# Transposing x by crossbar DMA in place of TensorE, in a convolution and token-mixing kernel

## The chip, the cores and the metric

One core of one Trainium2 chip. The metric is the device time of one execution in microseconds (us). Every time, ratio and profile in this document is from runs in the "fast" state, so no comparison mixes states; one of the four runs of h2_act (1607.5 us) was in the slow state and is left out. A "ratio" is the mean time of one kernel's runs over the mean of the other's runs of the same rounds, so it isn't quite the ratio of the medians that are quoted beside it.

Engines: PE is TensorE (matmul), PEld its weight loads, DVE VectorE, ACT ScalarE, POOL GpSimd. SPq is the SyncE queue that issues DMA. A crossbar transfer is a DMA with `transpose=True`. A transfer lands when its data have arrived; landing times are counted from its issue. A halo copy brings a chunk the 16 rows of history that its convolution needs. "L138" is line 138 of that kernel's file; the change moves later lines by some ten, so L408 of the kernel before is L417 of the changed one.

## The reference

```python
def _attn_ref(x, weight):                  # x (8, 4224, 192), weight (8 heads, 7 taps)
    w = softmax(weight)                    # cut: written out in the original
    x_pad = concat([zeros(6 rows), x])     # causal
    x_unf = x_pad[:, idx, :].reshape(B, S, K, H, group)
    return einsum('hk,bskhg->bshg', w, x_unf)

def _moe_ref(x, w_theta, w_tok_r, w_tok_i, w_ch):
    theta = x @ w_theta                                  # contracts over the channel
    zr, zi = x * cos(theta), x * sin(theta)
    y = einsum('ts,bsd->btd', w_tok_r, zr) + einsum('ts,bsd->btd', w_tok_i, zi)
    u = x + y
    return u + maximum(u @ w_ch, 0.0)                    # contracts over the channel
```

The large work is the token mixing: two 4224 x 4224 matrices times 1536 columns. The theta product contracts over the channel, and x comes out of the convolution with tokens on the partitions, so x must be transposed before it. That transpose is what the change touches.

## The kernel before

The 4224 tokens are 33 chunks of 128. A chunk is loaded, convolved, transposed, multiplied by `w_theta`, and turned into seven combinations z, which the mixing matmuls (`y`) read. Eleven chunks are alive at a time. Chunks 0 to 10 are prepared in an opening; chunks 11 to 32 are prepared in two later stages, spread as events between mixing matmuls. Preparation uses the PSUM pool "mm" (two buffers).

```python
    def transposed(u, by_dve=False):
        tp = banks("tp", F16)
        for k in range(6):
            pe(nc.tensor.transpose(
                tp[:, 0, k * P : (k + 1) * P], u[:, k * P : (k + 1) * P], ident))
        uT = wk.tile([P, 6, P], F16, name="uT", tag="uT")          # 2 buffers
        evacuate(uT[:, :, :].rearrange("p k s -> p (k s)"), tp[:, 0, 0 : 6 * P], by_dve)
        return uT

    class Chunk:
        def __init__(self, k, before=None):
            ...                                   # for a in range(4), a quarter each:
                if before is not None:            # 16 rows of history, SBUF to SBUF
                    nc.sync.dma_start(out=hist, in_=before.xw[lo + Q : lo + Q + HALO, h, :, :])
                ...
                nc.gpsimd.dma_start(out=self.xw[...], in_=x[...])  # x from HBM, cast to f16

        def conv(self, j):
            ...                                   # 8 matmuls, evacuated by ACT into self.x
            if j == 1:
                for a in range(NQ):
                    t0 = token(self.k, a)
                    nc.sync.dma_start(out=xs[t0 : t0 + Q, :], in_=self.x[a * Q : (a + 1) * Q, :])

        def transpose(self, g):                   # g = 0, 1: the two halves of the batch
            self.xT[g] = transposed(self.x[:, g * GC : (g + 1) * GC], ...)

        def theta(self, g):
            v = channel_mix(self.xT[g], wth)      # 8 matmuls on PE
            ...                                   # two sines on ACT into z

    # later chunks: places in a step, in sevenths of it, for
    # conv, conv, transpose, transpose, theta, theta, product, product, sums, sums
                pos = [0, .5, 1.3, 1.6, 2.1, 2.5, 3.1, 3.15, 3.4, 3.6]
                ...
                at += 2.3                         # the second chunk of the same step

    # the opening, iteration i: ch is chunk i, old is chunk i - 1; between(n) puts
    # mixing matmuls in between, as far as there are any
        ch.conv(0); between(2); old.theta(0); between(1); ch.conv(1)
        between(2); old.theta(1); between(1)
        ch.transpose(0); old.product(Z11); between(1)
        ch.transpose(1); old.product(Z21); ...
```

## Time and profile before

| | before |
|---|---|
| time | 1469.05 us median of 4 runs (1468.66 to 1469.96) |
| PE busy | 1434.6 us, 98% of the span |
| transposes of x on PE | 66 groups of six |
| landing of stores of x (96 KB, SP queue) | median 4.5 us from issue |

The chain of waits in order of time (start, duration, what), kernel before, in a later stage, and one long piece of it:

```profile
107.54 315.09 PE y L408 x1938
...
437.57 0.34 PE tp L153 x6
437.91 0.65 PE y L408 x4
438.56 0.34 PE tp L153 x6
438.89 1.62 PE y L408 x10
```

Six transposes cost the chain 0.34 us. The unbroken stretches of 315 and 296 us are useful landmarks: they hold no chunk work, so the time up to the first one's end is the opening, from there to the second one's end is the first later stage, and the rest follows.

### The profile page before, as it was taken

The page shows a single profiled execution, that of the slowest core. Times are in us where ns is not written, and L with a number is a line of the kernel's source. Part 1 is how long each engine was busy: PE and PEld are TensorE (multiplying, and loading weights), DVE is VectorE, ACT ScalarE, POOL GpSimd, SP SyncE. Part 2 cuts the span into 40 slices and gives each one's busy share as a digit, 9 for nine tenths or more (in the row PEclk, how much of TensorE's full clock was granted, in tenths as well). Part 3 has the DMA queues.
Part 4 walks back from the last instruction along what each step waited for, and adds up shares of the span by engine and source line. Part 5 has one row for each costly group of instructions (what it writes and reads, how often), then busy time and mean ns, then how long its engine had stood idle before and what let it go on. Part 6 is the DMA issues. An engine that isn't in the chain of part 4 may idle for free.

```text
span 1469.8 us, 24434 instructions
## 1 busy us (share of the span) xinstructions
PE 1434.6 (98%) x10095; PEld 905.6 (62%) x10095; DVE 1001.0 (68%) x1050; ACT 360.7 (25%) x461; POOL 430.3 (29%) x659
## 2 busy tenths in 40 slices
PE   7789999999999999999999999999999999999997
PEld 4556666666666666666666666666666666666665
DVE  6884655454548687766656658769777787778575
ACT  6861101111134353000000015254122222121224
POOL 7422211111223322211113232332233333453220
PEclk9999999999999999999999999999999999999998
DMA  9976756574699999887879989999778777999873
GB/s 172 227 155 145 144 104 144 96 151 89 149 232 212 232 224 263 193 198 167 209 162 239 200 194 229 201 232 256 128 191 197 173 182 185 224 237 217 196 201 108
DMA packets 234975, 274.16 MB, mean 187 GB/s; under 512 B 69104, under 2 KB 202608, under 8 KB 234864
## 3 DMA queue, kind: packets, MB, share of 16 engines
q0 software_dynamic: 163616, 95.30, 49.0%
q1 hardware_dynamic: 71248, 177.30, 34.1%
q8 instruction: 79, 1.29, 0.3%
q14 instruction: 32, 0.26, 0.1%
HBM read 245.49 MB, written 111.28 MB: 243 GB/s over the span
## 4 chain that ended last, share of the span: by engine, by line
PE 91%; DVE 3%; ACT 3%; DMA 1%; issue 1%; POOL 0%; DVEq 0%; ACTq 0%; POOLq 0%
PE y L408 81%; PE v L138 6%; PE tp L153 3%; ACT z L233 2%; PE pc L196 2%; DMA st<-in_moe_w_tok_i_dram 1%; DVE pv L373 1%; DVE z L244 1%; DVE z L238 0%; DVE wt L308 0%; DVE pv L437 0%; ACT uT L148 0%; DVE wt L320 0%; ACT pv L371 0%; ACT z L148 0%
## 5 line engine op out<-in xcount | busy, mean ns | idle before, releaser
L408 PE MATMUL y<-z,wt 128*128 128x384 f16 x7656 | 1295.3, 326 | 7.7 <-DVE pv L373 6.8
L408 PEld LDWEIGHTS <-wt 128*128 128x128 f16 x7656 | 737.5, 98 | 475.0 <-issue 10.4
L373 DVE TENSOR_TENSOR pv<-y,pv 128x768 f32<-128x768 f32 x324 | 308.5, 953 | 374.2 <-PE y L408 348.6
L308 DVE STREAM_TRANSPOSE wt<-st 128x1408 f16<-128x1408 f16 (+7 forms) x224 | 326.4, 1463 | 7.7 <-DMA st<-in_moe_w_tok_i_dram 7.0
L295 POOL DMA_DIRECT2D st<-in_moe_w_tok_i_dram x232 | 132.7, 581 | 497.7 <-DVE wt L308 473.7
L295 POOL DMA_DIRECT2D st<-in_moe_w_tok_r_dram x232 | 132.7, 581 | 459.0 <-DVE wt L308 443.7
L320 DVE TENSOR_TENSOR wt<-wt 128x1408 f16<-128x1408 f16 (+7 forms) x216 | 204.1, 945 | 9.5 <-PE y L408 6.6
L148 ACT ACTIVATE uT<-tp 128x768 f16<-128x768 f16 x127 | 102.3, 813 | 296.8 <-PE tp L153 294.9
L148 ACT ACTIVATE z<-pc 128x768 f16<-128x768 f32 x65 | 52.9, 814 | 386.5 <-PE pc L196 386.5
L371 ACT ACTIVATE pv<-y 128x768 f32<-128x768 f32 x66 | 53.7, 813 | 281.5 <-PE y L408 281.5
L138 PEld LDWEIGHTS <-uT 128*128 128x128 f16 x1056 | 93.0, 99 | 25.9 <-issue 9.9
L437 DVE SCALAR_TENSOR_TENSOR pv<-v,pv 128x768 f32<-128x768 f32 x66 | 62.7, 949 | 46.8 <-PE v L138 45.5
L183 POOL DMA_DIRECT2D xw<-in_x_dram x132 | 76.5, 591 | 35.8 <-issue 10.1
L427 ACT ACTIVATE ub<-pv 128x768 f16<-128x768 f32 x66 | 54.8, 837 | 90.6 <-DVE pv L373 89.5
L244 DVE TENSOR_TENSOR z<-z 128x768 f16<-128x768 f16 x132 | 73.4, 556 | 3.8
L233 ACT ACTIVATE z<-v,half_pi 128x768 f16<-128x768 f32 x66 | 59.6, 903 | 40.0 <-PE v L138 39.8
L238 DVE TENSOR_TENSOR z<-z 128x1536 f16<-128x1536 f16 x66 | 60.4, 950 | 10.8 <-ACT z L233 10.8
L355 POOL TENSOR_TENSOR pv<-pv,xr 128x1536 f32<-128x1536 f32 x20 | 62.9, 3144 | 7.9 <-issue 4.5
L138 PE MATMUL v<-wch,uT 128*128 128x192 f16 x528 | 56.9, 254 | 3.5 <-DVE pv L437 1.9
L138 PE MATMUL v<-wth,uT 128*128 128x192 f16 x528 | 54.3, 246 | 3.1 <-ACT z L233 3.0
L233 ACT ACTIVATE z<-v 128x768 f16<-128x768 f32 x66 | 53.2, 805 | 0.0
L153 PE MATMUL tp<-ident,z 128*128 128x128 f16 x396 | 33.4, 222 | 8.8 <-ACT z L233 8.3
(43 smaller groups left out, 201.5 us busy)
## 6 DMA issues: line engine op xcount, KB each, us to landing
part<-pv SPq DMA_DIRECT2D x79, 768.0 KB, 4.3
pv<-part SPq DMA_DIRECT2D x79, 768.0 KB, 5.4
out_dram<-pv SPq DMA_DIRECT2D x66, 384.0 KB, 4.5
st<-in_moe_w_tok_r_dram POOLq DMA_DIRECT2D x136, 176.0 KB, 5.8
st<-in_moe_w_tok_i_dram POOLq DMA_DIRECT2D x136, 176.0 KB, 4.9
xs<-z SPq DMA_DIRECT2D x132, 96.0 KB, 4.5
xw<-in_x_dram POOLq DMA_DIRECT2D x121, 96.0 KB, 5.9
part<-xs POOLq DMA_DIRECT2D x26, 384.0 KB, 7.4
```

The costliest lines, as they stand in the source:

```text
L138: pe(nc.tensor.matmul(v[:, k, b * D : (b + 1) * D], lhsT=tT[:, 3 * k + b + i, :], rhs=w[:, 2 * b + i, :], start=(i == 0), stop=(i == 1),))
L148: act(nc.scalar.activation(out=out, in_=in_, func=AT.Copy))
L153: pe(nc.tensor.transpose(tp[:, 0, k * P : (k + 1) * P], u[:, k * P : (k + 1) * P], ident))
L183: nc.gpsimd.dma_start(out=self.xw[lo : lo + n, h, :, :], in_=x[:, t0 : t0 + n, :].rearrange("b s d -> s b d"),)
L233: act(nc.scalar.activation(**args))
L244: dve(nc.vector.tensor_tensor(out=z[:, o, :], in0=z[:, a, :], in1=z[:, b, :], op=ALU.subtract))
L295: pool(nc.gpsimd.dma_start(out=st[a * Q : (a + 1) * Q, 0:nb, :, 0:n] .rearrange("i r bt s -> i (r bt) s"), in_=w[self.tbs[0] * P : (self.t ...
L308: dve(nc.vector.transpose(self.w[name][:, 0 : self.n, :, :], self.st[int(name[1])][:, int(name[0]) - 1, :, 0 : self.n * Q] .rearrange("p b ...
L320: dve(nc.vector.tensor_tensor(out=self.w[name][:, 0 : self.n, :, :], in0=self.w[a][:, 0 : self.n, :, :], in1=self.w[b][:, 0 : self.n, :, : ...
L355: pool(nc.gpsimd.tensor_tensor(out=self.pv[i], in0=self.pv[i], in1=xr, op=ALU.add))
L373: dve(nc.vector.tensor_tensor(out=o, in0=yv, in1=o, op=ALU.add))
L408: pe(nc.tensor.matmul(y[cn][:, q, 0:BH], lhsT=self.w[wn][:, c, :, :].rearrange("p bt i -> p (bt i)"), rhs=chunks[k].z[:, zn, q * BH : (q + ...
```

## The change

The intent is to take the 396 transposes of x from the bound engine and the evacuations from ACT, and to let the DMA crossbar do them, SBUF to SBUF. The stores of x go behind the transfers on the same queue, theta is moved later, uT gets four buffers, and `wt` gives up one to pay for it. The transposes of u at the end of the kernel stay on TensorE.

```diff
+    def turned():
+        return wk.tile([P, 6, P], F16, name="uT", tag="uT", bufs=4)
+
+    def crossed(u):
+        uT = turned()
+        nc.sync.dma_start(out=uT, in_=u, transpose=True)
+        return uT
...
-            if j == 1:
-                for a in range(NQ):              # the store, cut
+        def store(self):                         # the same four transfers
...
         def transpose(self, g):
-            self.xT[g] = transposed(
-                self.x[:, g * GC : (g + 1) * GC], 0 < self.k < 3 or (self.k, g) == (0, 1)
-            )
+            self.xT[g] = crossed(self.x[:, g * GC : (g + 1) * GC])
...
-            return wpool.tile([P, NW, NQ, Q], F16, name="wt", tag="wt", bufs=11)
+            return wpool.tile([P, NW, NQ, Q], F16, name="wt", tag="wt", bufs=10)
...
-                pos = [0, .5, 1.3, 1.6, 2.1, 2.5, 3.1, 3.15, 3.4, 3.6]
+                pos = [0, .4, .8, .81, .82, 2.6, 3.0, 3.6, 3.65, 3.9, 4.1]
...                                              # the opening, behind ch.conv(1):
+        if ch:
+            for g in range(NG):
+                ch.transpose(g)
+            ch.store()
...                                              # and away from their old places
-        if ch:
-            ch.transpose(0)
```

More of the change, by code (lines that the diff above doesn't have):

```diff
@@ L155, in transposed @@
             ))
-        uT = wk.tile([P, 6, P], F16, name="uT", tag="uT")
+        uT = turned()
         evacuate(uT[:, :, :].rearrange("p k s -> p (k s)"), tp[:, 0, 0 : 6 * P], by_dve)
@@ L209, in conv @@
             )
-            if j == 1:
-                for a in range(NQ):
-                    t0 = token(self.k, a)
-                    nc.sync.dma_start(
-                        out=xs[t0 : t0 + Q, :], in_=self.x[a * Q : (a + 1) * Q, :]
-                    )
+        def store(self):
+            for a in range(NQ):
+                t0 = token(self.k, a)
+                nc.sync.dma_start(
+                    out=xs[t0 : t0 + Q, :], in_=self.x[a * Q : (a + 1) * Q, :]
+                )
         def transpose(self, g):
-            self.xT[g] = transposed(
-                self.x[:, g * GC : (g + 1) * GC], 0 < self.k < 3 or (self.k, g) == (0, 1)
-            )
+            self.xT[g] = crossed(self.x[:, g * GC : (g + 1) * GC])
         def theta(self, g):
@@ L253, in tasks @@
                 yield lambda g=g: self.transpose(g)
+            yield self.store
             for g in range(NG):
@@ L642 @@
         between(1)
-        if ch:
-            ch.transpose(0)
         if old:
             old.product(Z11)
-        between(1)
-        if ch:
-            ch.transpose(1)
+        between(2)
         if old:
```

## The prediction

> **What bounds the kernel now.** TensorE: the page gives PE 98% busy of 1469.8 us, and the chain of waits is 91% PE. Busy time by windows shows PE full through nearly all of 150 to 1400 us. It falls short in the opening (36.0 of the first 50 us, 43.4 of the next) and at the end. Every TensorE instruction taken out of the dense part is real time. In the opening, where eleven chunks are prepared one after another, the chain alternates between PE, ACT and DVE, at 6.7 to 7.9 us a chunk.
>
> **What is removed.** 396 transposes of x, in 66 groups of six. The chain in order of time shows a group taking 0.34 us of PE in the dense part. All 66 make 22.4 us; the 44 of chunks 11 to 32 make 15 us. That is 1.5% at most. 66 evacuations of 0.81 us on ACT (five are 0.56 us on DVE) and 66 uses of the two "mm" PSUM slots also go. In the opening ACT is about 85% busy (42.7 of 50 us), so 1.6 us a chunk could matter: PE waits 8.3 us for a sine before a transpose.
>
> **What is added.** 66 crossbar transfers of 192 KB on the SP queue. No trace here has one. The Trainium skill, "VectorE: DVE Perf Modes", section "The three transpose paths", gives 1309 ns for one 128x128 by crossbar; no run here shows it. Ordinary transfers on this queue take a median 4.3 us (48 KB, SBUF to SBUF) to 4.6 us (stores of 96 KB) to land. My estimate, from those landings and the skill's figure (six tiles, partly parallel), is 5 to 8 us from x complete to the first xT landed, the second 1 to 3 us later.
>
> **What lies on the critical path.**
> - Later chunks: theta now comes 1.8 sevenths of a step (about 6.5 us, a step being 26.7 us) behind the transfers. That roughly covers one landing. I expect -15 us, with 0 to 10 us given back in stalls before theta.
> - Opening: theta(0) still follows in the next iteration. The timeline shows the x evacuation ending at 74.4 us and the next theta(0) at 78.4 us: 4.1 us of room, less than an estimated landing. [...] the shortfall stalls everything. The cycle theta, sine, evacuation, transfer, theta would be about 4.5 us plus the landing, 10 to 11 us instead of 7.7, over ten chunks: +15 to +35 us, after the removed work.
> - The stores of x move behind the transfers; nothing early needs them. wt with 10 buffers instead of 11: at most 9 or 10 are alive, so about 0.
>
> Sum: about +10 us, most likely 1479 us. Range 1442 to 1570. Faster by over 2% 0.04 (the ceiling is the 22 us plus part of 20 us of idle PE), within 2% 0.58, slower 0.38.
>
> **What would show it.** Right: the unbroken 300 us stretch of L408 in the chain starts later than the present 107.5 us; PE waits for DMA uT<-z before L138 in the first 110 us, 1 to 4 us each; between 420 and 580 us the step falls from 26.7 to about 25.4 us; the ACT group uT<-tp falls from 127 to 66. Wrong: no PE wait on uT in the opening (then about 1447 us), or waits of several us at nearly every theta in the dense part.
>
> **What would make it wrong.** A crossbar transfer much dearer than a plain one: at 8 us or more of the SP queue or the engines, two per 13 us fill it and hold up pv and halo loads: 1550 us or beyond. Or landing within 4 us, which leaves nearly the whole gain. A third risk: the added small packets delay the W loads.

## More of the kernel before

The kernel before was run again with each group of experiments, with medians of 1468.9 to 1470.5 us.

Engine totals, then three rows of the span cut into 40 slices (busy tenths; PEclk is the clock granted to TensorE; DMA is the mean busy share of the 16 DMA engines), then the DMA queues, from the page of the kernel before:

```profile
PE 1434.6 (98%) x10095; PEld 905.6 (62%) x10095; DVE 1001.0 (68%) x1050; ACT 360.7 (25%) x461; POOL 430.3 (29%) x659
...
PE   7789999999999999999999999999999999999997
...
PEclk9999999999999999999999999999999999999998
DMA  9976756574699999887879989999778777999873
...
q0 software_dynamic: 163616, 95.30, 49.0%
q1 hardware_dynamic: 71248, 177.30, 34.1%
```

PE is full except in the first three slices and the last. But the DMA row is at 9 in the same places where chunks are prepared: the first two slices, slices 12 to 16 and 25 to 28, among others. The quiet stretch from slice 3 to 11 is at 4 to 7. q1, the queue that the crossbar transfers will join, has 71,248 packets.

Busy time by windows (PE, PEld, DVE, ACT, POOL; then granted clock, DMA share, GB/s), kernel before: the opening, and the first later stage.

```profile
0.00:108.00 108.00, 86.33 (x774) 57.06 (x775) 84.36 (x137) 76.69 (x102) 54.63 (x105) 1.00 1.04 187
422.00:577.00 155.00, 154.27 (x1223) 99.00 (x1222) 116.96 (x141) 69.28 (x88) 46.37 (x82) 1.00 0.99 230
```

The DMA share is 1.04 and 0.99: it sums the queues' packet times, so it can pass 1.

## The result, and the profile after

The changed kernel takes 1527.97 us (median of 4, 1521.68 to 1531.41) against 1469.05: ratio 1.0395 (95% interval 1.0361 to 1.043), slower. Its output is correct.

The page of the changed kernel, same lines:

```profile
PE 1438.2 (94%) x9701; PEld 892.1 (58%) x9701; DVE 1001.0 (66%) x1045; ACT 314.4 (21%) x400; POOL 430.3 (28%) x659
...
PE   6669999999998998999999999898999999999997
...
PEclk9889999999999999999999999999899999999999
DMA  9997765656599999988788989999977787899974
...
q0 software_dynamic: 163616, 95.30, 47.9%
q1 hardware_dynamic: 124048, 190.29, 40.0%
```

394 instructions are gone from PE, and yet it is busy for 3.6 us longer. Its idle time (span less busy) went from 35.2 to 87.8 us. q1 moves only 13 MB more (66 times 192 KB), in 52,800 more packets, and its share of 16 engines rises from 34.1% of 1469.8 us to 40.0% of 1526.0 us. That is 109 us more, or an estimated 1.65 us of all 16 engines per transfer.

The same windows by stage, changed kernel, and two pieces of the chain:

```profile
0.00:130.00 130.00, 91.89 (x641) 55.91 (x642) 81.43 (x132) 64.94 (x85) 54.62 (x105) 0.88 1.15 190
445.00:619.00 174.00, 154.04 (x1096) 93.56 (x1096) 117.94 (x141) 51.69 (x66) 46.01 (x82) 0.97 1.12 226
```
```profile
130.06 315.08 PE y L417 x1938
...
485.49 10.21 DMA uT<-z
495.70 0.05 issue
495.74 0.88 PE v L138 x8
```

The first unbroken stretch begins at 130.1 us in place of 107.5. In the later stage the same work takes longer at a higher DMA share and a lower clock, and the chain now runs through a transfer that takes 10.21 us.

Who PE waited for (us in total, times, longest), and the issues and landings of the new tile, changed kernel:

```profile
PE v L138 <- DMA uT<-z: 63.4, 28, 8.1
...
L156 SPq DMA_TRANSPOSE uT<-z x66: 1211/1324/3937, 12.8 to 1073.7; - x66
...
DMA to landing us min/median/max: 2.5/6.4/12.3
```

63.4 us of the idle time is theta waiting for its own transposed x. A transfer takes 1.3 us to issue and a median 6.4 us to land, 12.3 at worst.

Why PE's busy time didn't fall is seen in PE's timeline around the longest wait (idle time in brackets) and in the windows there:

```profile
92.92 0.82 PE L417 MATMUL y<-z,wt 128*128 128x384 f16 x4
101.81 1.46 PE L138 MATMUL v<-wth,uT 128*128 128x192 f16 x8 [8.07 <-DMA uT<-z]
103.06 0.85 PE L417 MATMUL y<-z,wt 128*128 128x384 f16 x2
...
109.72 0.82 PE L417 MATMUL y<-z,wt 128*128 128x384 f16 x4
```
```profile
102.00:108.00 6.00, 6.00 (x35) 3.98 (x34) 1.98 (x2) 2.90 (x4) 0.18 (x1) 0.56 0.21 59
108.00:118.00 10.00, 8.97 (x76) 5.63 (x74) 9.40 (x14) 6.41 (x9) 2.72 (x5) 1.00 1.10 175
```

After the 8.07 us pause eight theta matmuls take 1.46 us instead of 0.82, and the granted clock of the next 6 us is 0.56; then it is back at 1.00. With these pauses the mean granted clock over the whole run fell from 0.996 to 0.980, which is some 24 us of 1526 by that figure. It agrees with the busy time: 22.4 us of transposes are gone and the sum is 3.6 us higher, so the rest became about 26 us slower. The Trainium skill, "TensorE: Matmul & The Clock Gate", section "Why this matters for your kernels", advises no PE-idle gaps of over about 3 us between matmul bursts. This trace agrees roughly. Of the waits for uT, those of 8.07, 4.59, 4.14, 3.54 and 3.08 us were followed by a theta of 1.46 us. Behind those of 4.58 and 3.09 us theta itself took 0.88 and 0.83 us, but what came next was slow: the clock of 496 to 500 us was 0.57, and eight matmuls of the convolution took 0.85 us in place of 0.52. Just below 3 us it goes both ways: two waits of 2.97 us were followed by slow matmuls, those of 2.94 and 2.88 us were not. One wait of only 1.56 us was followed by a theta of 1.46 us, but a pause of 1.82 us had ended 1.2 us before it began.

### The profile page after: what moved, and what is told of

It is laid out like the page before. It is cut to its first block, busy times and chain, and to the rows that moved or that the text cites. A ratio compares the mean times of both kernels' runs of the same rounds, so it can differ in the third digit from the quotient of the medians.

```text
span 1526.0 us, 23663 instructions
## 1 busy us (share of the span) xinstructions
PE 1438.2 (94%) x9701; PEld 892.1 (58%) x9701; DVE 1001.0 (66%) x1045; ACT 314.4 (21%) x400; POOL 430.3 (28%) x659
## 4 chain that ended last, share of the span: by engine, by line
PE 78%; DMA 14%; DVE 3%; ACT 2%; issue 1%; POOL 1%; SPq 0%; DVEq 0%; POOLq 0%; ACTq 0%
PE y L417 71%; DMA uT<-z 11%; PE v L138 5%; DMA xw<-in_x_dram 2%; ACT z L241 1%; PE tp L162 1%; PE pc L205 1%; DVE pv L382 1%; DMA st<-in_moe_w_tok_i_dram 1%; DVE z L252 1%; POOL st L304 1%; DVE wt L317 1%; DVE pv L446 0%; ACT z L148 0%; POOL xw L192 0%
## 5 line engine op out<-in xcount | busy, mean ns | idle before, releaser
L329 DVE TENSOR_TENSOR wt<-wt 128x1408 f16<-128x1408 f16 (+7 forms) x216 | 204.0, 944 | 22.1 <-PE y L417 18.2
L138 PEld LDWEIGHTS <-uT 128*128 128x128 f16 x1056 | 96.2, 104 | 97.0 <-DMA uT<-z 75.9
L138 PE MATMUL v<-wth,uT 128*128 128x192 f16 x528 | 65.1, 276 | 64.9 <-DMA uT<-z 63.4
L148 ACT ACTIVATE uT<-tp 128x768 f16<-128x768 f16 x66 | 53.2, 810 | 242.1 <-PE tp L162 242.1
L205 PE MATMUL pc<-xw,bands 96*64 96x192 f16 x528 | 38.5, 271 | 4.7 <-DMA xw<-in_x_dram 3.4
```

Of the source, the lines that this page charges most:

```text
L138: pe(nc.tensor.matmul(v[:, k, b * D : (b + 1) * D], lhsT=tT[:, 3 * k + b + i, :], rhs=w[:, 2 * b + i, :], start=(i == 0), stop=(i == 1),))
L148: act(nc.scalar.activation(out=out, in_=in_, func=AT.Copy))
L329: dve(nc.vector.tensor_tensor(out=self.w[name][:, 0 : self.n, :, :], in0=self.w[a][:, 0 : self.n, :, :], in1=self.w[b][:, 0 : self.n, :, : ...
```

## The experiments

The theories. **Wait**: theta stands too close behind a transfer that needs 6 us to land; with more distance PE would not wait and the 15 us of the later stages would be won. **Load**: the DMA engines are full where chunks are prepared; the transfers lengthen everything there, wherever theta stands. **Queue**: it is the SP queue, by its issue time (1.3 us a transfer) or by transfers waiting for earlier ones to land.

All with three rounds of the kernel before beside them. Stage columns are differences to the kernel before, worked out from the ends of the two unbroken stretches and the span of the profiled run (before: 422.6, 449.8 and 597.4 us), each good to some 0.1 us. By the 2% verdict e2, e7, h1 and h3 count as the same and e6 and g3 as unclear, but the 95% interval of every ratio lies above 1.

| run | median us | ratio | up to the end of stretch 1 | to the end of stretch 2 | rest |
|---|---|---|---|---|---|
| the change | 1528.0 | 1.0395 | +22.5 | +18.3 | +15.3 |
| e2_opening_only | 1491.1 | 1.0144 | +23.5 | 0.0 | -4.4 |
| e3_later_only | 1503.0 | 1.0224 | +0.8 | +18.2 | +12.2 |
| e4_unread | 1518.7 | 1.0337 | +17.5 | +16.5 | +9.3 |
| e7_copy | 1489.6 | 1.0140 | +13.4 | +1.6 | +2.5 |
| g1_unread_halo | 1508.6 | 1.0270 | +18.8 | +9.2 | +9.8 |
| g2_halo | 1527.7 | 1.0386 | +22.4 | +18.7 | +15.5 |
| e6_far_open_pe | 1500.7 | 1.0206 | -0.3 | +12.6 | +18.2 |
| g3_far_halo_open_pe | 1497.6 | 1.0195 | +0.8 | +9.6 | +13.8 |
| h1_quiet | 1484.1 | 1.0102 | +13.4 | 0.0 | -0.6 |
| h2_act | 1585.4 | 1.0816 | +38.1 | +38.7 | +37.1 |
| h3_half | 1480.3 | 1.0087 | +0.8 | +3.5 | +5.0 |
| c256 | 1514.4 | 1.0284 | +20.5 | +15.2 | +8.6 |

### Which stage: e2_opening_only and e3_later_only

```diff
-            self.xT[g] = crossed(x)
+            self.xT[g] = crossed(x) if self.k < NW else transposed(x)      # e2
+            self.xT[g] = crossed(x) if self.k >= NW else transposed(x, ...) # e3
```
In each, the part that went back to TensorE also went back to its places of before.

> The crossbar for chunks 0 to 10 only; chunks 11 to 32 are transposed on TensorE at the places of before. By the markers of the two traces the opening alone ends 22.5 us later in the changed kernel, so 1491 us if the stages add up. If the loss sat in the later stages through the shared queue, this stays near 1470.

> The reverse: the opening as before, the crossbar for chunks 11 to 32 at the places of the change. The markers give +34.6 us for the two later stages, so 1503 us if the stages add up. My prediction had 1454 to 1464 for this half (-15 us and 0 to 10 us of stalls).

They gave 1491.1 us (ratio 1.0144) and 1503.0 us (1.0224). The stages add up roughly: about 21 and 33 us, of the 59 of the whole. (The 34.6 us in the second expectation don't agree with the table: the markers give 18.3 and 15.3.) The opening's loss is of the size predicted. The later stages' is not: 33 us lost, where 5 to 15 us of gain was predicted.

One more effect shows here. e2 has no crossbar after the opening, and yet its rest is 4.4 us shorter than before. It has four buffers of uT, which the transposes of u at the end use too. From the end of the last mixing matmul to the end of the span it is 18.0 to 19.3 us in all four profiles with two buffers of uT (the kernel before, e4, g1 and h1) and 14.4 to 15.0 us in all ten with four. So the change gains some 4 us at its end, which the prediction didn't have, and its transfers cost that much more; no run changed the buffers alone.

### The transfers without anyone waiting for them: e4_unread

```diff
+    def unread(u):
+        uX = wk.tile([P, 6, P], F16, name="uX", tag="uX", bufs=2)
+        nc.sync.dma_start(out=uX, in_=u, transpose=True)
 ...                                    # kernel before, wt with 10 buffers, in conv(1):
             if j == 1:
+                for g in range(NG):
+                    unread(self.x[:, g * GC : (g + 1) * GC])
                 for a in range(NQ):    # the stores, as before
```

> The kernel before, all transposes on TensorE, plus all 66 crossbar transfers at the places of the change, into tiles that nobody reads, stores of x behind them, wt with 10 buffers. Theory of the wait (theta stands too close behind a transfer that needs 6 us to land): nothing waits, so 1469 to 1476 us. Rival, contention (the transfers load the SP queue and the DMA engines and hold up halo copies, x loads and weights): 1500 us or more, with PE waiting for xw or wt.

1518.7 us (ratio 1.0337): some 48 us for transfers that nobody reads. The theory of the wait alone falls here. The change loses 59 us although it saves an estimated 22.4 us of transposes, some 81 us in all; by this estimate 48 of them come without anyone waiting for uT, if the two parts add up. Who PE waited for, and the landings, in this run:

```profile
PE pc L200 <- DMA xw<-xw: 11.9, 6, 2.7
...
DMA to landing us min/median/max: 2.5/6.8/12.0
```

PE now waits for the halo copies of the next chunk, for outputs that DVE was late with, and so on. No single wait explains the loss; it is spread. In the profiled run idle time rose by 25.2 us and busy time by 18.2 us, the latter with the granted clock at 0.983. One flaw: the unread tiles had two buffers only, so the SP queue itself waited 15.0 us for them.

### The same bytes as a plain copy: e7_copy

```diff
-        nc.sync.dma_start(out=uT, in_=u, transpose=True)
+        nc.sync.dma_start(out=uT[:, :, :].rearrange("p k s -> p (k s)"), in_=u)
```

> Wrong result on purpose: the changed kernel with a plain SBUF to SBUF copy of the same 192 KB in place of each crossbar transfer, all places and waits the same. If the crossbar itself is dear (256-byte packets), a copy lands in about 4.5 us against a median 6.4 us and the time falls to about 1485 us. If any transfer on this busy queue takes as long, it stays at 1525 to 1530 us.

1489.6 us (ratio 1.0140), and a wrong result as intended (relative error 0.04). Places, waits and bytes are those of the change; only the kind of transfer differs, and 38 of the 59 us are gone. The later stages lose 1.6 and 2.5 us in place of 18.3 and 15.3. The opening still loses 13.4 of 22.5 us: with 4.1 us of room there, a plain copy (median 5.6 us) is late as well. Queues, issues and landings of this run:

```profile
q1 hardware_dynamic: 80752, 190.28, 36.1%
...
L156 SPq DMA_DIRECT2D uT<-z x66: 470/550/2162, 12.8 to 1036.3; - x66
...
DMA to landing us min/median/max: 2.1/5.6/8.8
```

By the same arithmetic as above, a copy costs an estimated 0.54 us of all 16 engines (36 us over 66), a third of the crossbar's 1.65. The Trainium skill, "Advanced Engine Details and Errata", section "X-Bar Transpose (TRN2)", has transpose DMAs as fast as regular ones. In this kernel they aren't.

### Eight transfers in flight: g1_unread_halo and g2_halo

The generated program gives the SP queue's transfers eight completion semaphores in turn, so the ninth transfer waits until the first has landed. A chunk has two crossbar transfers, four stores and four halo copies; the program makes 33 of the 120 halo copies wait for a crossbar transfer in this way. Who the SP queue waited for, changed kernel:

```profile
SPq L183 <- DMA uT<-z: 26.7, 18, 3.1
```

The edit moves two quarters' history in one transfer, so that a chunk has eight:

```diff
                 if before is not None:
-                    nc.sync.dma_start(
-                        out=hist, in_=before.xw[lo + Q : lo + Q + HALO, h, :, :]
-                    )
+                    if h == 0:
+                        nc.sync.dma_start(
+                            out=self.xw[lo : lo + HALO, :, :, :],
+                            in_=before.xw[lo + Q : lo + Q + HALO, :, :, :],
+                        )
```

> The kernel with unread crossbar transfers (1518.7 us), its four halo copies of a chunk on the SP queue merged to two. In the program only eight transfers of the SP queue can be outstanding, the ninth waits until the first has landed, and the halo copies stand behind the crossbar transfers of the same chunk (2 transfers, 4 stores, 4 halo copies make ten). Theory of the slots: with eight in place of ten the halos no longer wait for the crossbar, PE no longer waits for the halos, 1480 to 1495 us. Theory of the DMA engines (256-byte packets crowd everything): 1510 us or more.

> The changed kernel (1528 us) with the halo copies merged. Slots: 1495 to 1510 us, what is left being the waits of theta for its own transfer. If only those waits matter, or only the DMA engines: 1520 to 1530 us.

1508.6 us (ratio 1.0270, against 1.0337) and 1527.7 us (1.0386, against 1.0395). The mechanism exists and cost e4 about 10 us, but most of e4's loss remains, and the change itself gains nothing. I had expected far more of it.

### More distance: e6_far_open_pe and g3_far_halo_open_pe

Both keep the opening on TensorE. Both chunks of a step are convolved and sent first; theta comes 2.5 and 3.1 sevenths of a step after the transfers in place of 1.8. g3 also has the merged halo copies.

```diff
-                pos = [0, .4, .8, .81, .82, 2.6, 3.0, 3.6, 3.65, 3.9, 4.1]
+                pos = ([0, .4, .8, .81, .82, 3.3, 3.7, 4.3, 4.35, 4.6, 4.8],
+                       [1.0, 1.4, 1.8, 1.81, 1.82, 4.9, 5.3, 5.9, 5.95, 6.2, 6.4])[c]
...
-                at += 2.3
```

> The opening on TensorE; for chunks 11 to 32 the crossbar, with theta moved further behind: both chunks of a step are convolved and sent first, theta comes 2.5 and 3.1 sevenths of a step (9 and 11 us) later in place of 1.8 (6.5 us). Theory of the wait: the 1503 us of the later-only kernel fall to 1455 to 1465 us. If contention is the larger part: 1480 us or more.

> The same with the halo copies merged as well. If both causes are right this has neither: 1455 to 1460 us, 10 to 15 us faster than before, the 44 groups of transposes at 0.34 us saved. If it stays at 1470 us or above, something else eats the saved TensorE time.

1500.7 us (ratio 1.0206) and 1497.6 us (1.0195), against 1.0224 at the old places: almost none of the 33 us comes back, and the 95% intervals overlap with that of e3. The landings show where the distance went. The three lines are, in this order, of e3_later_only, e6_far_open_pe and g3_far_halo_open_pe:

```profile
DMA to landing us min/median/max: 3.9/6.3/10.6
```
```profile
DMA to landing us min/median/max: 2.6/7.8/12.8
```
```profile
DMA to landing us min/median/max: 2.6/8.3/13.6
```

Four transfers sent together land later than two. With more distance given, the landing itself grew by 1.5 to 2 us. PE still waited 25.9 us for uT in e6 and 28.6 us in g3, against 31.7 in e3.

### A place where the DMA engines have room: h1_quiet

```diff
+        if 6 <= t < 16:                       # kernel before, wt with 10 buffers
+            def probe(g, t=t): ...            # unread tile, source z of chunk 0
+                if t < 11: nc.sync.dma_start(out=uX, in_=u, transpose=True)
+                else:      nc.sync.dma_start(out=uX[...], in_=u)      # plain copy
+            for at in (1.0, 4.5):
+                for g in range(NG): found.append((at + g / 100, ...))
```

> The kernel before plus 20 unread crossbar transfers, four in each of the steps 6 to 10, and 20 plain copies of the same 192 KB in the steps 11 to 15; there the DMA engines are about 60% busy. Theory of the engines' throughput (a crossbar transfer holds all 16 engines some 1.7 us: the hardware queue's share went from 34.1% of 1469.8 us to 40.0% of 1526.0 us for 66 of them; 0.5 us for a copy): the crossbar lands in 3 to 4 us, a copy in about 2.5 us, the DMA share rises by about 0.27 in the first steps and 0.08 in the others, and the time stays at 1470 us, as there is room. If a crossbar transfer costs PE something by its mere presence, the time rises by 10 us or more.

1484.1 us (ratio 1.0102), not the 1470 expected of room, nor quite what the rival said. The design was flawed: nothing held the probes back, so the SP queue ran ahead with them. Its timeline in this run:

```profile
27.33 10.87 SPq L493 DMA_TRANSPOSE uX<-z  x4
38.30 0.54 SPq L174 DMA_DIRECT2D xw<-xw  x1
41.64 1.22 SPq L493 DMA_TRANSPOSE uX<-z  x1
...
97.01 2.59 SPq L493 DMA_TRANSPOSE uX<-z  x2
...
109.86 24.08 SPq L493 DMA_TRANSPOSE uX<-z  x10
```

By accident it still tells two cases apart. Five transfers fell into the middle of the opening: the SP queue stood for 10.9 us over four of them, halo copies came behind, and PE waited 11.1 us for one; the opening's end moved by 13.4 us. So this loss looks like one of order on the queue, and isn't a test of the engines' throughput. Seven more came in the last 24 us of the opening. Eight crossbar transfers and all 20 copies were issued within the unbroken stretch that begins at 120.9 us. That stretch lasts 315.08 us as it does elsewhere, and from its end to the end of the second the kernel takes exactly what it took before (difference 0.0 us). Here the crossbar was free, and not because the engines had room: over its first 25 us, with the eight crossbar transfers, the DMA share was 1.21, against 0.71 over the first 25 us of the same stretch in the kernel before, and PE was busy for 25.00 us in both. In this stretch no chunk is prepared, so PE has less that hangs on a transfer. The same 0.0 us, with 10 buffers of `wt`, shows that the lost buffer costs PE nothing from that stretch on.

### The queue that issues: h2_act

```diff
-        nc.sync.dma_start(out=uT, in_=u, transpose=True)
+        act(nc.scalar.dma_start(out=uT, in_=u, transpose=True))
```

> The changed kernel with the crossbar transfers issued from the ACT queue. Rival, the SP queue (a crossbar transfer takes 1.3 us to issue, two a chunk, and stands behind stores that wait): the time falls from 1528 to below 1505 us. Engines' throughput: the same transfers on the same engines, 1515 to 1535 us.

1585.4 us (ratio 1.0816), the fourth run, slow, left out: worse than either theory said. ACT, which makes x and the sines, now issues the transfers between them, at a median 1.42 us each; PE waited 98.1 us for uT. What in this made it so much worse wasn't followed up. So it doesn't clear the SP queue's issue time as a part of the cause; it only shows that moving the issue isn't a cure.

The run has one more use: the crossbar transfers have a queue of their own here, q10.

```profile
q1 hardware_dynamic: 71248, 177.30, 34.0%
q10 hardware_dynamic: 52800, 12.98, 6.6%
```

6.6% of 1583.7 us over 66 is 1.58 us of all 16 engines per transfer, without a subtraction, near the 1.65 estimated above. But q1, with the same 71,248 packets as the kernel before, took 34.0% of 1583.7 us in place of 34.1% of 1469.8 us, 37 us more: the other packets' times were longer too, so the figures by subtraction are rough.

### Half the dose: h3_half

```diff
-            self.xT[g] = crossed(x) if self.k >= NW else transposed(...)
+            self.xT[g] = crossed(x) if self.k >= NW and g == 0 else transposed(...)
...
-                pos = [0, .4, .8, .81, .82, 2.6, 3.0, 3.6, 3.65, 3.9, 4.1]
+                pos = [0, .4, .8, 1.6, 1.61, 2.6, 3.0, 3.6, 3.65, 3.9, 4.1]
```

> Opening on TensorE; of each later chunk one half by crossbar (22 transfers), the other on TensorE: half the dose of the later-only kernel (1503 us, +33). Throughput of engines that are already full: about half, 1480 to 1490 us. A wait that only the second transfer of a pair causes: 1463 to 1470 us, as the first alone lands in time.

1480.3 us (ratio 1.0087): 22 transfers cost about 11 us net, 44 cost about 33. The second half of the dose costs about twice the first. PE waited 15.7 us for uT, so the first transfer of a pair is late too, and half a dose doesn't pay either.

### The packets: c256

A plain copy again, but cut into pieces of 256 bytes by padding uT.

```diff
-        return wk.tile([P, 6, P], F16, name="uT", tag="uT", bufs=4)
+        return wk.tile([P, 6, P + 8], F16, name="uT", tag="uT", bufs=4)[:, :, 0:P]
...
-        nc.sync.dma_start(out=uT, in_=u, transpose=True)
+        nc.sync.dma_start(out=uT, in_=u.rearrange("p (k s) -> p k s", s=P))
...                          # the evacuation on the TensorE path, fitted to the new shape
```

> Wrong result on purpose: the changed kernel with a plain copy in place of each crossbar transfer, as before (1489.6 us with 1536-byte rows), but cut into pieces of 256 bytes, six a partition, 768 a transfer, as many as the crossbar has. If the small packets are what loads the engines: 1515 to 1530 us, like the crossbar (1528), and the share of the hardware queue rises from 36.1% to about 40%. If it is the crossbar itself, or its 1.3 us of issue on the SP queue: about 1490 us, like the copy with long rows.

1514.4 us (ratio 1.0284), wrong result as intended. Queues, issues and landings:

```profile
q1 hardware_dynamic: 122992, 190.28, 37.3%
...
L156 SPq DMA_DIRECT2D uT<-z x66: 599/664/1545, 12.8 to 1058.5; - x66
...
DMA to landing us min/median/max: 2.6/6.2/11.8
```

The same bytes in 256-byte pieces cost 25 us more than in long rows, with an issue of 0.66 us, near the copy's 0.55. The Trainium skill, "DMA: Bandwidth & Descriptors", section "Specifications", gives 512 B as the least for line rate; that pieces of 256 bytes cost more agrees with it, but no run here tried 512. Those 25 us are about two thirds of the distance from the copy to the crossbar (1489.6, 1514.4, 1528.0 us). The last third is the crossbar itself or its longer issue; these runs don't separate the two. The estimated engine time per transfer goes the same way: 0.54, 0.96 and 1.65 us.

## Why the prediction was right or wrong

The time, 1528 us, lies inside the range of 1442 to 1570, and "slower" had a chance of 0.38. But the most likely value was 1479 us, 49 us short; "within 2%" had been given the larger chance, 0.58, and one of the two main terms had the wrong sign. That the time fell inside is owed to a range of 128 us and is luck more than insight.

- **What PE saves**: right in size. 0.34 us a group was a trace figure, and 66 groups left PE. The gain was eaten: busy time rose by 3.6 us.
- **The landing**: right. "5 to 8 us" from x complete; the median from issue is 6.4 us. The spread up to 12.3 us wasn't foreseen.
- **The opening**: right in mechanism and size. +15 to +35 us was said; the markers give +22.5 us, e2 about 21 us, with PE waiting 0.8 to 8.1 us before theta, where 1 to 4 us was said. e7_copy sharpens it: 13.4 us of this would befall any transfer at that place.
- **The later stages**: this is the step that failed. "I expect -15 us, with 0 to 10 us given back" was in truth +18.3 and +15.3 us by markers, about 33 us by e3. The mis-sized term is the give-back: about 48 us in place of 0 to 10, and some 4 more with the gain of the uT buffers taken out. The step of 26.7 us became 27.9 and 32.1 us in the first two of that stage (from the chain), not 25.4. Of the 44 thetas of these stages 18 waited for uT, 36.0 us in all, and e4 shows that more than waits is lost. I took the landing as a fixed delay that distance covers. e6 and g3 show that it isn't fixed: give more distance and send more at once, and it grows.
- **The third risk** ("the added small packets delay the W loads") was named and given no microseconds in the sum. It pointed at the right place. In the first later stage the DMA share went from 0.99 to 1.12, and the x loads' median landing from 6.8 to 9.3 us; 66 transfers of an estimated 1.65 us came to engines whose share already was 0.99 to 1.04 where chunks are prepared.
- **The clock**: not in the prediction at all. With the PE pauses the granted clock went from 0.996 to 0.980 on average, by the estimate above worth about as much as all the saved transposes.
- **wt with 10 buffers**: right, 0 us from the first unbroken stretch on (h1_quiet; its opening can't say).

What is shown: the transfers cost time by their presence (e4), more in packets of 256 bytes than in long rows (e7, c256), next to nothing beside the unbroken stretch (h1), and more distance, as tried here, doesn't repay them (e6, g3). That the DMA engines' throughput is the limit where chunks are prepared, since there PE soon needs what is being transferred, is the explanation that fits all of this, together with the shares; a full DMA share alone isn't enough (h1). No run here took away other DMA work there to prove it, and the SP queue's order has a part: some 10 us in e4 (g1), none seen in the change itself (g2). Also open: what the last 14 us from c256 to the crossbar are, and whether the transposes of u in the last stage, where the DMA share is 0.73 to 0.94 in the changed kernel by stretches of 100 us from 1100 to 1400 us, could go by crossbar with profit. No version run here beats the kernel before.

## What to carry to other kernels

Before giving DMA a job of the bound engine, read the DMA share of the very stage that the job falls in, and cost the new transfers by packet size and not by bytes alone; if the stage is already at 1.0 and its own work hangs on transfers, don't count on the landing time as a constant that more distance hides. Two cheap experiments settle such a case early: issue the new transfers unread beside the old code, and put plain copies of the same bytes in their place. And when TensorE loses its steady feed, count its clock as well as its waits.

## What the Trainium skill lacked or had wrong

- "Advanced Engine Details and Errata", "X-Bar Transpose (TRN2)": transposes as fast as regular DMAs. Here 192 KB took an estimated 1.65 us of the 16 engines by crossbar, 0.54 us as a copy in long rows and 0.96 us as one in pieces of 256 bytes; in the same places the crossbar and the copy in long rows made a kernel of 1528 against 1490 us.
- "VectorE: DVE Perf Modes", "The three transpose paths": one figure, 1309 ns for 128x128 by crossbar, and no word on the load beside it. A 128x768 transfer landed in 2.5 us at best and 6.4 us at the median, 12.3 at worst, beside other traffic. The page gives nothing on how the time grows with load.
- "DMA: Bandwidth & Descriptors" gives the issue of a crossbar transfer from SBUF only in cycles of "previous generations" beside a later chip, for another shape. Here 128x768 took 1.3 us to issue on the SP queue, against 0.55 us for a copy.
- "TensorE: Matmul & The Clock Gate", section "Why this matters for your kernels": the 3 us gap is a fair guide, since here slow matmuls followed all seven waits of 3.08 us and more within 1.1 us; but they also followed two waits of 2.97 us, while none followed those of 2.94 and 2.88 us, and the row says nothing of two short pauses close together (1.82 and 1.56 us here), which had the same effect.
